# An attention and mixture-of-experts kernel on one core: the second group's second product turned round, zeros placed freely, and the engines' order planned with other durations

## The chip, the core and the metric

The kernel runs on one NeuronCore of a Trainium2 chip. The metric is the device time of one execution in microseconds; the number to be predicted is the median of the timed runs of the changed kernel.

## What is computed

Two steps in float32. First chunked attention: 4 batches, 8 heads, 768 positions, head dimension 64; every chunk of 32 queries sees 8 memory keys, 16 keys to its left, its own 32 and 8 to its right. Its output, 3072 rows (tokens) of 512, is the input of the second step, a dense mixture of 4 experts:

```python
scores = scale * np.matmul(q_c, k_full.transpose(0, 1, 3, 2))
a = np.exp(scores - np.max(scores, axis=-1, keepdims=True))
a = a / (np.sum(a, axis=-1, keepdims=True) + 1e-09)
out[:, :, c_start:c_end] = np.matmul(a, v_full)
...
p = domain_probs / (domain_probs.sum(-1, keepdims=True) + 1e-09)
for e in range(E):                       # E = 4
    h = np.maximum(x @ w1[e], 0.0)       # 3072 x 512 by 512 x 1024
    out += p[:, e:e + 1] * (h @ w2[e])   # 3072 x 1024 by 1024 x 512
```

## The kernel before

**Groups and experts.** A group is one batch, 768 tokens in two halves of 384. The work is numbered by n = 4 * group + expert, from 0 to 15. While a group is multiplied with the weights, attention of the next group runs between (`window`, `attend`): one unit is 96 queries, with a score product (L485), a mixing product (L618) and the softmax on VectorE (DVE) and ScalarE (ACT).

**Products.** Each float32 matrix is split into a high part (a cast to fp32r on ACT, L550) and a low part (what is left, a subtraction on DVE, L568, or on GpSimd (POOL), L569; `parts_of`). A product is three matmuls: high by high, high by low, low by high. From expert 1 on the first product (L883) is a Strassen-like product of seven half-sized products (named 11, 12, 6, 5, 7, 4, 3 after their steps), worked off in four pairs p of hidden blocks per expert; class `Full` takes the sums, rectifies them (`relu`, `direct`) and splits them again as operands of the second product.

**The second product** is again seven products of half size, in two forms. `Halves` (L1123) has the hidden layer's 128 tokens as the stationary operand and 256 output columns moving by: three token blocks t, so steps 10, 11, 12, 20 and so on; its sums are weighted with the routes p as they are added up (`add_up`, L837, 256 columns). `Across` (L1167) has the weights as the stationary operand and 384 tokens moving by: two steps t per product; the result stands with the model dimension on the partitions, so the routes are multiplied onto the hidden layer before (`weigh`, L983; for pairs 0 and 1 a rectification on ACT, L552, and a product on POOL or DVE), from a broadcast copy that `want_routes` loads, and the sums (384 columns) are plain additions. `FLAT` is the first group that uses `Across`. In `Halves` the steps 10 and 11 write PSUM banks of kind `a` (two of these) and 12 a bank of kind `moe` (three); in `Across` steps 10 and 11 both write kind `a`. The kind `a` banks also hold the first product's sums: the fourth pair's bank is read last after step 4 (`direct`: the rectification on ACT in groups with `Halves`, `weigh` on DVE in groups with `Across`). Step 3 of the fourth pair (product S4) comes between step 4 and the next step of the second product.

**The start.** The first group's attention and first products are laid out by hand in `FIRST_BLOCK`: S is a unit's scores, T its transposes (L1350), X its mixing (L1369), M and N first products (L817), g and G second products of the first expert (L863), and W n matmuls of zeros (L1270) on idle data, which keep TensorE (PE) at work.

**The order of the engines.** Nothing else is ordered by hand. `Plan` records every operation with its reads and writes. PE's order is that of the program; for ACT, DVE, POOL and the queue of SyncE (SP), which issues all DMAs, `run` draws orders at random around due times, replays each with modelled durations, and keeps the best; an addition or subtraction may be on DVE or POOL, a copy on ACT or DVE, as it finds best. There are three plans: the start ("first"), groups' work up to expert 3 ("mid"), and all from n = 4 on ("fin").

## Time and profile before

| what | value |
|---|---|
| timed runs | 1043.56, 1045.62, 1047.1 us (median 1045.62) |
| span of the profiled execution, first to last instruction | 1041.7 us |
| mean granted clock of PE | 0.997 |
| DMA moved | 300.88 MB, mean 289 GB/s |
| start (first plan) | 0 to 72.4 us |
| first group and expert 3 (mid) | to 305.8 us |
| second group, n = 4 to 7, `Halves` | 305.8 to 559.3 us |
| third and fourth group, n = 8 to 15, `Across` | 559.3 to 1038.3 us |

The profiled execution has no time of its own beside its span; the timed runs lie 1.9 to 5.4 us above it. In the profile, PE is the matmuls and PEld the weight loads beside them. A row of the timeline has the start, the length, the engine, the line, output and inputs, the shapes (a matmul's stationary operand, then its output) and how many instructions are merged; in square brackets stand the idle time before it and who ended it. A row of a group has busy time, mean length in ns, and idle time before with its releasers. Matmuls overlap in their pipeline, so that a matmul's length is longer than its distance to the next.

### The profile page before, as it was taken

The numbers are of one execution on the slowest core, as the hardware profiler recorded it, in microseconds if no ns is written. First come the engines' busy times: TensorE is split into PE (matmuls) and PEld (weight loads), VectorE is DVE, ScalarE is ACT, GpSimd is POOL, SyncE is SP. The second block draws the span as 40 slices with busy tenths as digits, with TensorE's granted clock in tenths as the row PEclk, the third lists the DMA queues.
The fourth block names the chain that finished last, engine by engine and source line by source line (L and its number), as shares of the span: only waits on it lengthen the run. The fifth ranks groups of instructions, "written<-read, shape, count | busy, mean of one in ns | idle before, by whom it ended". The sixth has DMA issues, their size and how long they took to land.

```text
span 1041.7 us, 21404 instructions
## 1 busy us (share of the span) xinstructions
PE 1030.7 (99%) x7899; PEld 988.8 (95%) x7899; DVE 809.4 (78%) x1358; ACT 539.3 (52%) x1426; POOL 464.9 (45%) x426
## 2 busy tenths in 40 slices
PE   7999999999999999999999999999999999999998
PEld 6988988989889999999999999999999999999998
DVE  6869786868976768678797968969699765949485
ACT  5636864746737656474755546445453534334241
POOL 2444654854605436172253606346072634626172
PEclk8999999999999999999999999999999999999999
DMA  9557989989979999999988878879679887879784
GB/s 297 179 206 238 376 335 359 357 333 352 347 279 384 357 306 333 326 342 328 309 259 303 282 259 278 279 246 296 232 241 305 287 262 247 280 237 275 250 253 144
DMA packets 185512, 300.88 MB, mean 289 GB/s; under 512 B 14816, under 2 KB 125504, under 8 KB 185408
## 3 DMA queue, kind: packets, MB, share of 16 engines
q1 hardware_dynamic: 185408, 299.51, 84.4%
q8 instruction: 63, 1.03, 0.4%
q14 instruction: 41, 0.34, 0.1%
HBM read 230.21 MB, written 69.26 MB: 287 GB/s over the span
## 4 chain that ended last, share of the span: by engine, by line
PE 93%; DVE 4%; DMA 1%; issue 1%; POOL 0%; ACT 0%; SPq 0%; DVEq 0%; POOLq 0%; ACTq 0%
PE a_ps L883 22%; PE moe_ps L883 16%; PE moe_ps L863 13%; PE a_ps L1167 12%; PE moe_ps L1167 10%; PE a_ps L1123 7%; PE moe_ps L1123 5%; PE moe_ps L817 3%; PE x_ps L618 2%; PE s_ps L485 2%; DVE A_lo L568 1%; DVE u L983 1%; DVE u L568 1%; DMA raw<-in_w_dram 1%; DMA qk_pair<-in_qk_dram 1%
## 5 line engine op out<-in xcount | busy, mean ns | idle before, releaser
L569 POOL TENSOR_TENSOR u<-u,routes 128x384 f32<-128x384 f32 x46 | 50.3, 1095 | 191.8 <-ACT u L552 191.5
L568 DVE TENSOR_TENSOR A_lo<-u,A_hi 128x384 fp32r<-128x384 f32 x139 | 118.2, 868 | 18.8 <-ACT A_hi L550 18.4
L863 PE MATMUL moe_ps<-w,h_hi 128*128 128x512 f32 x384 | 119.8, 393 | 0.0
L568 DVE TENSOR_TENSOR u<-moe_ps,u 128x384 f32<-128x384 f32 x120 | 66.2, 552 | 63.4 <-PE moe_ps L883 48.3
L569 POOL TENSOR_TENSOR raw<-raw 128x256 f32<-128x256 f32 x57 | 51.2, 899 | 127.1 <-DMA raw<-in_w_dram 83.1
L550 ACT COPY u<-a_ps 128x384 f32<-128x384 f32 x120 | 57.0, 475 | 78.8 <-PE a_ps L883 77.1
L550 ACT CAST A_hi<-u 128x384 fp32r<-128x384 f32 x144 | 73.3, 514 | 37.5 <-DVE u L983 31.1
L863 PEld LDWEIGHTS moe_ps<-w,h_hi 128*128 128x128 f32 x384 | 71.1, 188 | 14.8
L883 PE MATMUL a_ps<-xc_hi,ring 128*128 128x384 f32 x384 | 82.2, 336 | 0.0
L552 ACT ACTIVATE u<-u 128x384 f32<-128x384 f32 x96 | 50.2, 525 | 53.3 <-DVE u L568 52.7
L863 PE MATMUL moe_ps<-w,h_lo 128*128 128x512 f32 x192 | 75.0, 391 | 0.0
L569 POOL TENSOR_TENSOR us<-u,u 128x384 f32<-128x384 f32 x43 | 49.4, 1149 | 41.8 <-DVE u L983 20.3
L883 PEld LDWEIGHTS a_ps<-xc_hi,ring 128*128 128x128 f32 x384 | 67.8, 188 | 0.0
L1167 PE MATMUL a_ps<-A_hi,ring 128*128 128x384 f32 x256 | 65.8, 338 | 0.6 <-DVE u L983 0.6
L569 POOL TENSOR_TENSOR us<-u,us 128x384 f32<-128x384 f32 x43 | 49.5, 1151 | 30.2 <-DVE us L568 23.7
L569 POOL TENSOR_TENSOR u<-u,u 128x384 f32<-128x384 f32 x48 | 59.8, 1246 | 0.6
L569 POOL TENSOR_TENSOR u<-u,us 128x384 f32<-128x384 f32 x46 | 58.2, 1266 | 2.7 <-DVE A_lo L568 1.1
L639 ACT ACTIVATE s_sb<-s_ps,mx 96x64 f32<-96x64 f32 x192 | 57.1, 309 | 0.7
L568 DVE TENSOR_TENSOR acc<-a_ps,acc 128x384 f32<-128x384 f32 x52 | 28.8, 553 | 26.7 <-PE a_ps L1167 26.1
L883 PE MATMUL a_ps<-xc_lo,ring 128*128 128x384 f32 x192 | 48.9, 336 | 0.0
L1167 PEld LDWEIGHTS a_ps<-A_hi,ring 128*128 128x128 f32 x256 | 45.8, 188 | 2.4 <-DVE u L983 2.2
L569 POOL TENSOR_TENSOR w<-raw,w 128x512 fp32r<-128x512 f32 x25 | 35.9, 1443 | 26.7 <-ACT w L550 17.6
(237 smaller groups left out, 3110.8 us busy)
## 6 DMA issues: line engine op xcount, KB each, us to landing
ring<-k SPq DMA_DIRECT2D x144, 512.0 KB, 4.8
ring<-t SPq DMA_DIRECT2D x96, 512.0 KB, 6.0
ring<-w SPq DMA_DIRECT2D x72, 512.0 KB, 5.4
k<-w SPq DMA_DIRECT2D x48, 512.0 KB, 5.3
w<-w SPq DMA_DIRECT2D x32, 512.0 KB, 5.5
raw<-in_w_dram SPq DMA_DIRECT2D x62, 256.0 KB, 5.2
ring<-k SPq DMA_DIRECT2D x48, 256.0 KB, 4.1
qk_t<-in_qk_dram SPq DMA_DIRECT2D x24, 464.0 KB, 6.3
```

Source lines behind the costliest of these rows:

```text
L485: nc.tensor.matmul(s_ps.ap[c * CH:(c + 1) * CH, j * NPAIR + g, 0:KW], lhsT=x()[rows, g * UQ + c * CH:g * UQ + (c + 1) * CH], rhs=x()[rows, ...
L550: nc.scalar.copy(out(), x())
L552: nc.scalar.activation(out(), x(), func)
L568: ("DVE", t_dve(cols), lambda: nc.vector.tensor_tensor(out=out(), in0=x(), in1=y(), op=op)),
L569: ("POOL", t_pool(cols), lambda: nc.gpsimd.tensor_tensor(out=out(), in0=x(), in1=y(), op=op)),
L618: nc.tensor.matmul(x_out()[j * D:(j + 1) * D, g, :], lhsT=v_t.ap[:, h * D:(h + 1) * D], rhs=aT[:, j * NPAIR + g, :], start=True, stop=True,)
L639: now["plan"].add("ACT", t_act(KW) + 0.08, lambda h=h: nc.scalar.activation(s_sb.ap[:, h, :], s_in()[:, h, :], AF.Exp, bias=mx.ap[:, h, :] ...
L817: nc.tensor.matmul(ps.ap[:, lo:hi], lhsT=a[:, c * P:(c + 1) * P], rhs=x[:, c, lo:hi], start=(i == 0), stop=(i == len(steps) - 1),)
L863: nc.tensor.matmul(self.ps.ap, lhsT=h.ap[:, self.rows], rhs=w.ap[:, part, :], start=(i == 0 and k == 0), stop=(i == NF - 1 and k == 2),)
L883: nc.tensor.matmul(ps.ap[:, 0:SG], lhsT=a()[:, c * P:(c + 1) * P], rhs=y[:, k0 + c, :], start=(first and i == 0), stop=(i == len(steps) - ...
L1123: nc.tensor.matmul(ps.ap[:, cols], lhsT=x.ap[:, rows], rhs=w_ap[:, y, :], start=(begins and k == 0 and i == 0), stop=(k == NP2 - 1 and i = ...
L1167: nc.tensor.matmul(ps.ap[:, 0:SG], lhsT=w_ap[:, y, rows], rhs=x.ap, start=(begins and k == 0 and i == 0), stop=(k == NP2 - 1 and i == 2), ...
```

## The change

Four things change.

1. `FLAT` is 1 instead of 2: the second group (n = 4 to 7) uses `Across` too. The host puts the outputs of three groups, not two, back in order.
2. `FIRST_BLOCK` has other numbers and places of zeros (79 in all, before 98), in pieces of four, and another order of first products and transposes.
3. The planner's durations: latencies by engine and direction, the full wait of a DVE operation with two SBUF inputs for a running POOL operation and the other way round (`LOCK`), the end of an instruction hidden under the next (`OVER`), and single costs of PE and ACT work.
4. The planner plans in windows of 10 to 15 us with a limited sight instead of the whole plan at once, carries the state of three replays with it, and judges a window by PE's end and a little by the other engines'.

A way to fuse exponential and sum at the start (`FUSED`) is written but used by no unit.

```diff
-FLAT = 2
+FLAT = 1
...
-FIRST_TURNS, FIRST_SEED = 600, 1
+FIRST_TURNS, FIRST_SEED = 100, 1
 FIRST_BLOCK = """
-W32 S0 S1 S2 W6 S3 W30 T0 W6 X0 T1 W12 X1 S4 W12 M1 T3 M5 X3 M2 T2 S5 X2 S6 M6 N7 N5 N4 N6 N0 N2 T5 N1 N3 S7 X5
-g0 T4 g1 G0 X4 T7 G1 X7 T6 g2 X6 G2
+W31 S0 S1 W4 W4 S2 W4 W4 S3 W4 T0 W4 W4 W4 X0 T1 W4 W4 X1 W4 W4 S4 M6 M5 T3 M2 X3 T2 M1 X2 S5 S6 N1 N3 S7 N6 N7
+N4 N5 N0 T5 T4 N2 X4 g0 G0 X5 T7 g1 G1 T6 X7 g2 X6 G2
 """
...
-LATENCY = 0.12
-LATENCY_PE = 0.2
+LOCK = 0.14
+LATENCY = {"PE": 0.055, "ACT": 0.035, "DVE": 0.035, "POOL": 0.08, "SP": 0.12}
+BEYOND = {"PE": 0.165, "ACT": 0.0, "DVE": 0.0, "POOL": 0.0, "SP": 0.085}
+SELF = {"PE": 0.0, "ACT": 0.02, "DVE": 0.02, "POOL": 0.05, "SP": 0.12}
+OVER = {"PE": 0.0, "ACT": 0.1, "DVE": 0.08, "POOL": 0.04}
...
+HOPS = {"first": (15.0, 400.0, 60.0), "mid": (10.0, 160.0, 60.0), "fin": (10.0, 60.0, 30.0)}
+TRAIL = 0.05
...
 def t_pool(cols):
-    return 0.35 + cols * 0.0021
+    return 0.185 + cols * 0.00216
...
-                if op.two and start < pool_to:
-                    time += 0.9 * min(pool_to - start, time)
                 if op.two:
+                    time += max(0.0, pool_to - start - LOCK)
                     dve_to = start + time
             elif e == "POOL":
-                if start < dve_to:
-                    time += 0.25 * min(dve_to - start, time)
+                time += max(0.0, dve_to - start - LOCK)
                 pool_to = start + time
...
+                score = sum(f["PE"] + TRAIL * sum(max(0.0, f[e] - f["PE"]) for e in ("ACT", "DVE", "POOL"))
+                            for f, _ in ends) / len(ends)
...
-            pe(1.0, scores(s_ps, lambda: qk_t.ap), [qk_t], [s_ps])
+            pe(0.72, scores(s_ps, lambda: qk_t.ap), [qk_t], [s_ps])
...
-            now["plan"].add("ACT", t_act(KW) + 0.08, lambda h=h: nc.scalar.activation(
+            now["plan"].add("ACT", t_act(KW) + 0.147, lambda h=h: nc.scalar.activation(
...
-        pe(0.111 * n, fn, [], [])
+        pe(0.107 * n, fn, [], [])
```

The lines of the changed kernel are numbered anew: L1123 is L1204, L1167 is L1248, L883 is L964, L983 is L1064, L568 and L569 are L649 and L650.

What the change moves, at three places. The first is PE at the second product of the first expert of the second group (n = 4): the end of the third step of the fourth pair, product 1's step 10, steps 4 and 3 of the fourth pair, and the next step of product 1. `xa`, `xb` and `xc` are the parts of the input, `ring` the weights, `A_hi` and `A_lo` the parts of the hidden layer. Before:

```order
L883 MATMUL a_ps<-xc_lo,ring 128x384 x2
L1123 MATMUL a_ps<-ring,A_hi 128x256 x2
L1123 MATMUL a_ps<-ring,A_lo 128x256
...
L883 MATMUL a_ps<-xb_hi,ring 128x384 x4
L883 MATMUL a_ps<-xb_lo,ring 128x384 x2
L883 MATMUL moe_ps<-xb_hi,ring 128x384 x4
L883 MATMUL moe_ps<-xb_lo,ring 128x384 x2
L1123 MATMUL moe_ps<-ring,A_hi 128x256 x2
L1123 MATMUL moe_ps<-ring,A_lo 128x256
```

With the change:

```order
L964 MATMUL a_ps<-xc_lo,ring 128x384 x2
L1248 MATMUL a_ps<-A_hi,ring 128x384 x2
L1248 MATMUL a_ps<-A_lo,ring 128x384
...
L964 MATMUL a_ps<-xb_hi,ring 128x384 x4
L964 MATMUL a_ps<-xb_lo,ring 128x384 x2
L964 MATMUL moe_ps<-xb_hi,ring 128x384 x4
L964 MATMUL moe_ps<-xb_lo,ring 128x384 x2
L1248 MATMUL a_ps<-A_hi,ring 128x384 x2
L1248 MATMUL a_ps<-A_lo,ring 128x384
```

The step behind the fourth pair writes an `a` bank where it wrote a `moe` bank; operands change places and 256 columns become 384. In the whole program 1008 matmuls of 256 columns are gone and 672 of 384 have come.

The second place is PE in the first 25 us: scores (`qk_pair`), transposes of the bands (`band_107` for even units, `band_109` for odd ones), mixing (`v_t`), and the first products (`xa_hi`). The rows left out between them are the zeros: before, 6, 30, 6, 12 and (behind the fifth score) 12.

```order
L485 MATMUL att_ps<-qk_pair 32x64 x72
...
L485 MATMUL att_ps<-qk_pair 32x64 x24
...
L1350 MATMUL att_ps<-ident,band_107 128x96 x8
...
L1369 MATMUL x_ps<-aT_111,v_t 64x96 x8
L1350 MATMUL att_ps<-ident,band_109 128x96 x8
...
L1369 MATMUL x_ps<-aT_113,v_t 64x96 x8
L485 MATMUL att_ps<-qk_pair 32x64 x24
...
L817 MATMUL moe_ps<-xa_hi,w_359 128x192 x8
L817 MATMUL moe_ps<-xa_lo,w_359 128x192 x4
L1350 MATMUL att_ps<-ident,band_109 128x96 x8
```

With the change the zeros left out are 8, 8, 4, 12, 8 and 8:

```order
L566 MATMUL att_ps<-qk_pair 32x64 x48
...
L566 MATMUL att_ps<-qk_pair 32x64 x24
...
L1438 MATMUL att_ps<-ident,band_107 128x96 x8
...
L1457 MATMUL x_ps<-aT_111,v_t 64x96 x8
L1438 MATMUL att_ps<-ident,band_109 128x96 x8
...
L898 MATMUL moe_ps<-xa_hi,w_342 128x192 x8
L898 MATMUL moe_ps<-xa_lo,w_342 128x192 x4
L898 MATMUL moe_ps<-xa_hi,w_352 128x192 x8
L898 MATMUL moe_ps<-xa_lo,w_352 128x192 x4
L1438 MATMUL att_ps<-ident,band_109 128x96 x8
```

The third score stands behind eight zeros, four zeros instead of thirty stand in front of the first transpose, and two blocks of first products instead of one in front of the third transpose.

The third place is DVE in the last expert (n = 15), around the end of the fourth pair; `u11`, `u12`, `u21` and `u22` are sums of the first product, `A12_lo` and `A22_lo` low parts of the hidden layer, `acc` sums of the second product. Before:

```order
L568 TENSOR_TENSOR u22_12781<-a_ps_12705,u22_12781 128x384
L983 SCALAR_TENSOR_TENSOR u21_12674<-u21_12674,routes_12251 128x384
L983 SCALAR_TENSOR_TENSOR u22_12781<-u22_12781,routes_12251 128x384
L568 TENSOR_TENSOR A22_lo_12823<-u22_12601,A22_hi_12702 128x384
L983 SCALAR_TENSOR_TENSOR u12_12836<-a_ps_12705,routes_12215 128x384
```

With the change:

```order
L649 TENSOR_TENSOR u22_12436<-a_ps_12364,u22_12436 128x384
L649 TENSOR_TENSOR A12_lo_12471<-u12_12411,A12_hi_12421 128x384
L1064 SCALAR_TENSOR_TENSOR u22_12436<-u22_12436,routes_11958 128x384
L1064 SCALAR_TENSOR_TENSOR u21_12329<-u21_12329,routes_11958 128x384
L649 TENSOR_TENSOR acc_131<-a_ps_12458,acc_131 128x384
L1064 SCALAR_TENSOR_TENSOR u12_12495<-a_ps_12364,routes_11873 128x384
```

The last row of each is the weighing that frees the fourth pair's `a` bank; the lower part that stood right in front of it is another one further up, and a sum of the second product stands there now. Counted over the whole program, 44 low parts `A_lo` of 139 go from DVE to POOL, and of the sums and products with routes some 125 go from POOL to DVE or come new on DVE; DVE has 1342 rows with the change and 1294 before, POOL 430 and 431.

More of the change, by code (lines that the diff above doesn't have):

```diff
@@ L1 @@
 import random
+from bisect import bisect
 from contextlib import ExitStack
@@ new lines, in run, with judge @@
+        self.assign(self.ways)
+        free, dma, _, _, end = copies[0]
+        for op in ops:
+            op.end = end[op.index]
+        self.done = {**free, "DMA": dma}
+        self.score = self.judge([({**c[0], "DMA": c[1]}, max(c[4])) for c in copies])
+        self.emit(order)
+    def judge(self, ends):
+        total = 0.0
+        for free, most in ends:
+            if self.last:
+                total += most
+            elif not self.ahead:
+                total += free["PE"]
+            else:
+                total += max(free["PE"], free["SP"] + self.ahead, free["DMA"] + DMA_FIRST, *(free[e] - BEHIND for e in ("ACT", "DVE", "POOL")))
+        return total / len(ends)
@@ L266, in pushed @@
             for _ in range(rng.randrange(2, 14)):
-                need = [d for d in op.deps if d.engine != "PE"]
+                need = [d for d in op.deps if d.engine != "PE" and d in start]
                 if not need:
@@ L308, in replay, with schedule @@
-        return free["PE"] + (max(0.0, free["SP"] + self.ahead - free["PE"]) if self.ahead else 0.0)
-    def schedule(self, bias, ways):
+            else:
+                free[e] = start + time - OVER[e]
+            most = max(most, end[op.index])
+        return {**free, "DMA": dma}, most, (free, dma, pool_to, dve_to, end)
+    def schedule(self, place, base, bias, ways, stop, inside):
         self.assign(ways)
-        ops, wait = self.ops, self.wait
-        for op in ops:
+        wait = self.wait
+        waiting = {e: [] for e in ENGINES}
+        for op, left, ready in base:
@@ L324, in choose @@
+            waiting[op.engine].append(op)
+        for e in ENGINES[1:]:
+            waiting[e].sort(key=lambda o: (o.late, o.index))
+        free, at, line = dict(place["free"]), place["at"], self.line
+        dma, pool_to, dve_to, drift = place["dma"], place["pool_to"], place["dve_to"], place["drift"]
+        order, left = [], len(base)
+        everything = stop >= len(line)
         def choose(e, force):
```

188 lines of the change are left out of this document (119 added, 69 removed).

## The prediction

> **What bounds the kernel now.** I read the page first, then the waits of TensorE (PE), the windows, the timeline of PE at its stages, and last the groups by shape. The page's busy row and its chain of work:
>
> ```profile
> PE 1030.7 (99%) x7899; PEld 988.8 (95%) x7899; DVE 809.4 (78%) x1358; ACT 539.3 (52%) x1426; POOL 464.9 (45%) x426
> ...
> PE 93%; DVE 4%; DMA 1%; issue 1%; POOL 0%; ACT 0%; SPq 0%; DVEq 0%; POOLq 0%; ACTq 0%
> ```
>
> PE is busy for all but 11 us of the span of 1041.7 us, and it is 93% of the chain. So two things can shorten the kernel: fewer or cheaper matmuls, and the 11 us. The waits of PE and the windows say where these lie (after the stretch's length, the busy time of PE, PEld, DVE, ACT, POOL; then PE's granted clock):
>
> ```profile
> PE att_ps L485 <- DMA qk_pair<-in_qk_dram: 1.8, 1, 1.8
> PE att_ps L485 <- issue: 1.7, 1, 1.7
> PE x_ps L1369 <- ACT aT L563: 1.4, 2, 0.8
> PE x_ps L1270 <- POOL idle L455: 1.0, 1, 1.0
> PE att_ps L1350 <- ACT band L550: 0.6, 1, 0.6
> PE a_ps L1167 <- DVE u L983: 0.6, 2, 0.3
> PE att_ps L1350 <- POOL band L569: 0.3, 1, 0.3
> ...
> 0.00:20.00 20.00, 14.76 (x310) 13.17 (x310) 11.48 (x21) 8.81 (x17) 5.48 (x12) 0.83 0.87 275
> 20.00:40.00 20.00, 18.32 (x306) 16.90 (x304) 18.46 (x35) 16.75 (x37) 10.60 (x8) 1.00 0.79 283
> 40.00:80.00 40.00, 40.00 (x324) 35.33 (x324) 29.94 (x58) 14.22 (x28) 14.35 (x14) 1.00 0.47 168
> ```
>
> The first 40 us hold 6.9 us of PE's idle time; from 40 us on PE is full, but for 0.6 us at one kind of place (L1167) and the last sum's drain. Busy time hides waits shorter than a matmul's pipeline, so behind 40 us I go by distances from start to start.
>
> **The turn of the second product.** Two stretches of PE, one in the second group (256 columns) and one in the last (384):
>
> ```profile
> 349.73 0.40 PE L1123 MATMUL a_ps<-ring,Sb_hi 128*128 128x256 f32 x2
> ...
> 351.17 0.40 PE L1123 MATMUL a_ps<-ring,Sb_hi 128*128 128x256 f32 x2
> ...
> 1034.46 0.51 PE L1167 MATMUL moe_ps<-Sb_hi,ring 128*128 128x384 f32 x2
> ...
> 1036.54 0.51 PE L1167 MATMUL moe_ps<-Sb_hi,ring 128*128 128x384 f32 x2
> ```
>
> From the first to the second row lie 12 matmuls: (351.17 - 349.73)/12 = 0.120 us for 256 columns, (1036.54 - 1034.46)/12 = 0.1733 us for 384. By the code an expert has 7 products of 3 token blocks, 4 pairs and 3 terms, 252 matmuls of 256 columns; turned it has 7 x 2 x 4 x 3 = 168 of 384. Both stream 64,512 columns, and what is saved is the fixed part of 84 matmuls. For four experts: 1008 x 0.120 = 121.0 us go, 672 x 0.1733 = 116.5 us come: **-4.5 us**. PE is the chain there, so all of it counts.
>
> [...]
>
> What the turn lays on the other engines, by the groups of the second and third group's stretches:
>
> ```profile
> L837 DVE SCALAR_TENSOR_TENSOR acc<-a_ps,pr,acc 128x256 f32<-128x256 f32 x40 | 19.1, 477 | 7.0 <-PE a_ps L1123 6.7
> L983 DVE SCALAR_TENSOR_TENSOR u<-u,routes 128x384 f32<-128x384 f32 x24 | 19.0, 796 | 0.3
> L983 DVE SCALAR_TENSOR_TENSOR u<-a_ps,routes 128x384 f32<-128x384 f32 x16 | 8.8, 548 | 1.8 <-PE a_ps L883 1.8
> L568 DVE TENSOR_TENSOR acc<-a_ps,acc 128x384 f32<-128x384 f32 x26 | 14.3, 552 | 7.7 <-PE a_ps L1167 7.4
> ...
> 431.60:494.50 62.90, 62.90 (x551) 62.10 (x550) 48.06 (x89) 36.55 (x103) 27.40 (x27) 1.00 0.98 340
> 621.00:683.00 62.00, 62.00 (x468) 61.02 (x467) 50.10 (x86) 28.97 (x86) 26.66 (x24) 1.00 0.84 269
> ```
>
> Per expert of the second group the routes are now put on the hidden layer: 6 weighings of 0.80 us and 4 of 0.55 come to VectorE, and 18 adds of 0.48 become 12 of 0.55: +4.8 + 2.2 - 8.6 + 6.6 = +5.0 us on 48.1 us (the first row of windows), so 53 of 62 us. The third group has run like this with 50.1 us of VectorE, and PE is full in both rows. ScalarE loses 10 rectifications per expert; 6 products with the routes come, for GpSimd or VectorE as the planner likes. Two broadcasts of the routes per expert (192 KB each) pass SP's queue, 0.4 MB where 340 GB/s (the row's last number) move 21 MB in 62.9 us. Beside PE all of this is hidden and costs 0; the cover is VectorE's 9 free us per expert, and were it gone, each missing us would be one of PE's.
>
> **One hand-over loses its cover.** Behind the fourth pair, product 1's next step follows product S4. Before, that step wrote a free `moe` bank; turned, it writes the `a` bank that the fourth pair's A22 product has just filled, and waits until VectorE has weighed it out (the rows of PE's order in the section on the change). Groups three and four show the price:
>
> ```profile
> 833.10 1.37 DVE L568 TENSOR_TENSOR A_lo<-u,A_hi 128x384 fp32r<-128x384 f32 x1
> ...
> 834.20 0.51 PE L883 MATMUL moe_ps<-xb_lo,ring 128*128 128x384 f32 x2
> 834.39 0.54 DVE L983 SCALAR_TENSOR_TENSOR u<-a_ps,routes 128x384 f32<-128x384 f32 x1
> ...
> 834.99 0.44 PE L1167 MATMUL a_ps<-A_hi,ring 128*128 128x384 f32 x1 [0.28 <-DVE u L983]
> ```
>
> PE's two matmuls from 834.20 on need 0.35 us, the next starts after 0.79: a wait of 0.44 us, because a lower part of 1.37 us (a sum of its size takes 0.55) stands ahead of the weighing. The eight experts of groups three and four pay 1.45 us there in all, read in this way: three nothing, five 0.14 to 0.44, of which the first and the last are
>
> ```profile
> 712.96 0.51 PE L883 MATMUL moe_ps<-xb_lo,ring 128*128 128x384 f32 x2
> 713.50 0.61 PE L1167 MATMUL a_ps<-A_hi,ring 128*128 128x384 f32 x2
> ...
> 1010.17 0.51 PE L883 MATMUL moe_ps<-xb_lo,ring 128*128 128x384 f32 x2
> 1010.95 0.62 PE L1167 MATMUL a_ps<-A_hi,ring 128*128 128x384 f32 x2 [0.27 <-DVE u L983]
> ```
>
>  Twelve experts pay it after the change. Ends: the new order removes all of it, -1.4 us; every expert pays the worst, 12 x 0.44 - 1.45 = +3.8 us. For the last expert the new VectorE order has a sum of 0.55 us in front of the weighing where a lower part stood, which shortens it, while four experts are added to it: I take **0**.
>
> **The first 40 us.** Rows of the timeline, and the clock:
>
> ```profile
> 10.54 1.96 ACT L550 COPY band<-s_sb 32x64 f32<-32x64 f32 x4 [1.20 <-DVE s_sb L1316]
> 12.61 3.38 PE L1270 MATMUL x_ps<-idle 128*128 128x128 bf16 x30
> 15.79 0.97 PE L1350 MATMUL att_ps<-ident,band 96*128 96x96 f32 x8
> ...
> 23.03 1.11 PE L817 MATMUL moe_ps<-xa_hi,w 128*128 128x192 f32 x8
> 25.25 0.88 PE L1350 MATMUL att_ps<-ident,band 96*128 96x96 f32 x8 [0.63 <-ACT band L550]
> 30.08 0.88 PE L1350 MATMUL att_ps<-ident,band 96*128 96x96 f32 x8 [0.28 <-POOL band L569]
> ...
> 10.00:12.00 2.00, 0.55 (x27) 0.31 (x14) 1.72 (x3) 1.44 (x4) 0.00 (x0) 0.50 1.02 385
> ```
>
> The band of unit 0 is whole at 12.50 us, but thirty matmuls of zeros stand in front of its transpose, which starts at 15.79 us: 3.3 us late. They were meant for time that the wait without a releaser (1.7 us, just before) had used up. The change leaves 4 zeros there, and 12 behind it. Two waits follow later, 0.63 us ahead of the transpose at 25.25 and 0.28 ahead of that at 30.08; the new order puts one more block of first products (over 1.1 us, the row at 23.03) in front of each. If everything moves up with the transpose the head gains 3.3 + 0.9 = 4.2 us. If VectorE decides, it gains little: from 20 to 40 us it is busy for 18.46, so only 1.5 us can be squeezed there, and the band's multiplication now stands behind the third score's maximum. The low end is a loss of 0.5 us, when a stretch without zeros keeps the clock at 0.50 (the last row) a little longer. I take **-2.0**, the free 1.5 us and a part of what is idle before 20 us, nearer to VectorE's row than to the transpose's. The waits for the first loads (1.8), for an instruction without a releaser (1.7) and for the zeros' memset (1.0) stay.
>
> **The rest of the order.** The planner's new durations and windows move nearly every instruction off PE, 44 lower parts among them to GpSimd and some 80 sums back to VectorE. Where PE was full it can gain nothing, so the sign can only be a loss; the hand-over above bounds it. The drain behind the last matmul stays.
>
> **The rivals.**
> 1. *The turn alone counts.* The head is VectorE's, nothing comes of the zeros: -4.5, 1041.1 us. For it speaks 18.46 of 20 us; against it the two waits that are covered without VectorE.
> 2. *Hand-overs at their worst.* Twelve waits of 0.44 us: -4.5 - 2.0 + 3.8 = -2.7, 1042.9 us. Five of eight experts show such a wait now.
> [...]
> 4. *Slower: the bank of the hand-over.* Where the weighing stands behind a whole contended lower part (1.37 us) in each of twelve experts, PE waits 12 x 1.37 - 1.45 = 15.0 us more: 1045.6 - 6.5 + 15.0 = 1054.1 us. It eats the gain from (6.5 + 1.45)/12 = 0.66 us per hand-over on, and is slower by 0.3% from 0.92 us on. Against it: the worst of eight is 0.44.
>
> That the change does not do what it says is out: its order has no matmul of 256 columns left and 672 more of 384.
>
> **How the numbers follow.** -4.5 + 0 - 2.0 = -6.5 us, a span of 1035.2 us. The timed runs (1043.56 to 1047.1 us, median 1045.62) lie 1.9 to 5.4 us above the span; no time of the profiled execution's own is given, so I carry the difference over to the median: **1039.1 us**. Chances: the forecast 0.60, rival 1 0.16, rival 2 0.11, rival 3 0.04, rival 4 0.09. About 0.3% (3.1 us) is what a measurement of this kernel can tell from no change. The forecast and most of rival 1 are faster by more: 0.75; rivals 2 and 3 and the rest of 1 are within: 0.16; rival 4: 0.09. The range goes from the head's better end and half the hand-overs, 1036, to just past rivals 1 to 3, 1043.8.
>
> **What would show it.** Right: 384-column matmuls 0.173 us apart where the second group ran 0.120, that group's four experts together some 4 us shorter; the first transpose near 13 us, PE full some 2 us earlier; a total of waits at the hand-over of 0 to 3 us. Wrong: a first M product no earlier than 23 us (the head), waits over 0.66 us each for the weighing (rival 4), or waits of PE for other lower parts between 70 and 560 us, where now there are none.

## The result, and the profile after

The changed kernel takes **1049.6 us** (median of five runs, 1048.2 to 1050.0) beside 1044.4 us (1043.1 to 1047.1) of the kernel before on the same chip: a ratio of 1.0047, 95% interval 1.0032 to 1.0062. It is slower by some 5.2 us where the prediction had 6.5 us gained; the time lies above the range. The profiled execution took 1048.4 us and has a span of 1046.6 us, 4.9 us more than that of before.

The page of the changed kernel, the busy row and the chain of work:

```profile
PE 1027.9 (98%) x7544; PEld 982.4 (94%) x7544; DVE 811.7 (78%) x1391; ACT 525.2 (50%) x1384; POOL 487.2 (47%) x431
...
PE 74%; DVE 14%; DMA 5%; issue 3%; POOL 2%; ACT 1%; SPq 0%; DVEq 0%; ACTq 0%; POOLq 0%
```

PE has less work, as meant, but the chain is now PE for only 74% (93% before): 14% of it passes through VectorE and 5% through DMAs. The waits of PE (line waited for: us in total, times, longest) say at which places:

```profile
PE a_ps L964 <- DMA ring<-k: 3.1, 2, 2.4
PE att_ps L566 <- issue: 2.2, 1, 2.2
PE a_ps L1248 <- DVE u L1064: 2.2, 4, 1.2
PE x_ps L699 <- DVE aT L742: 1.5, 2, 1.3
PE att_ps L566 <- DMA qk_pair<-in_qk_dram: 1.1, 1, 1.1
PE a_ps L964 <- DVE u L649: 1.0, 2, 0.6
PE x_ps L1351 <- POOL idle L536: 1.0, 1, 1.0
PE moe_ps L1248 <- DVE acc L649: 0.8, 1, 0.8
```

Three of these rows belong to the start and were there before (the first loads, the memset, `issue`). New are the ring of weights and many kinds of waits for VectorE, between 300 and 900 us, where before had 0.6 us. By stages, from the first matmul of each (the second group from the first product of expert 4 to that of expert 8, and so on; a group's last products come behind the next one's first, so that before's second group ends here at 555.7 us and in the table ahead of the prediction at 559.3):

| stage | before | after | difference |
|---|---|---|---|
| start, to the first product of the second half | 72.4 | 69.3 | -3.1 |
| first group, to expert 4 | 233.4 | 236.1 | +2.7 |
| second group | 249.9 | 252.1 | +2.2 |
| third group | 245.5 | 249.4 | +3.9 |
| fourth group and drain | 240.5 | 239.7 | -0.8 |

The start did move. PE's timeline there, the first transposes and the first M product:

```profile
13.03 0.87 PE L1438 MATMUL att_ps<-ident,band 96*128 96x96 f32 x8
...
21.01 1.14 PE L898 MATMUL moe_ps<-xa_hi,w 128*128 128x192 f32 x8
```

They are 2.8 and 2.0 us earlier than before. At the end of the first group most of it is gone again:

```profile
302.63 0.39 PE L944 MATMUL moe_ps<-w,h_lo 128*128 128x512 f32 x1
305.41 0.98 PE L964 MATMUL a_ps<-xa_hi,ring 128*128 128x384 f32 x4 [2.39 <-DMA ring<-k]
```

PE is done with the first group at 303.0 us and waits 2.4 us for the first weights of the next; before, it came to this place at 305.8 us and found them there. The turned products run as forecast:

```profile
359.87 0.51 PE L1248 MATMUL a_ps<-Sa_hi,ring 128*128 128x384 f32 x2
...
361.43 0.51 PE L1248 MATMUL a_ps<-A_hi,ring 128*128 128x384 f32 x2
```

There are nine matmuls from the first row to the second, (361.43 - 359.87)/9 = 0.173 us each. So the second group's matmuls are 4.5 us shorter, and the group is 2.2 us longer: 6.7 us are lost in it beside the matmuls. For 5.0 us of these PE is idle in the windows below (the length less PE's busy time); its waits there are 0.7 us for the ring, 0.7 us for ScalarE and 3.6 us for VectorE. What the other engines do in groups two and three (windows; after the length the busy time of PE, PEld, DVE, ACT, POOL, then PE's clock, DMA share and GB/s), before:

```profile
305.83:555.74 249.91, 249.87 (x2182) 246.31 (x2181) 194.54 (x338) 148.58 (x410) 105.78 (x99) 1.00 0.95 325
555.74:801.21 245.47, 245.44 (x1811) 241.40 (x1809) 202.38 (x341) 122.83 (x349) 105.27 (x89) 1.00 0.84 273
```

and after:

```profile
305.41:557.52 252.11, 247.11 (x1845) 240.65 (x1845) 208.59 (x355) 129.24 (x355) 130.87 (x117) 1.00 0.97 328
557.52:806.91 249.39, 247.27 (x1810) 241.86 (x1809) 200.76 (x347) 126.65 (x360) 110.39 (x91) 1.00 0.84 267
```

In the second group VectorE has 14 us more and GpSimd 25 us more: 39 us, or 9.8 us per expert, where the prediction had counted 5.0 us on VectorE and left GpSimd's part without a price. This is busy time, in which operations of either engine also take longer beside the other's (VectorE's product with the routes at 402.36 us 3.84 us, the one at 407.62 us, while GpSimd rests, 0.56 us; GpSimd's `Sa_lo` at 599.00 us, through which VectorE works without a break, 2.20 us, the one at 402.83 us 1.01 us), and not all of it is the turn's: the new planner moves lower parts to GpSimd, where they take longer (1.18 us on average for 0.78 on VectorE), and the same group unturned has 312 to 337 us on the two in the four runs below that have the new planner, for 300 us before. The turn alone, with the old planner, brings it to 352 us, 12.8 us more per expert:

```profile
304.40:565.40 261.00, 249.58 (x1845) 241.56 (x1845) 215.60 (x349) 128.95 (x355) 136.00 (x123) 0.99 0.94 318
```

The third group, which was taken as the proof that a turned group runs without waits, had 308 us on the two together before; the turned second group has 340 us, and its DMAs are full (0.97 against 0.84; 0.95 in the second group of before). What the second group has and the third has not are the sums of weights that experts 4 to 6 make for later products (`raw`). The groups of VectorE and of GpSimd in the second group after:

```profile
L649 DVE TENSOR_TENSOR raw<-raw 128x256 f32<-128x256 f32 x16 | 10.0, 624 | 1.7 <-POOL raw L650 1.6
L649 DVE TENSOR_TENSOR raw<-raw,t_hi 128x512 fp32r<-128x512 f32 x9 | 7.7, 859 | 0.1
...
L650 POOL TENSOR_TENSOR raw<-raw 128x256 f32<-128x256 f32 x16 | 14.0, 875 | 9.1 <-DVE raw L649 6.0 <-DMA raw<-in_w_dram 2.9
L650 POOL TENSOR_TENSOR raw<-raw,t_hi 128x512 fp32r<-128x512 f32 x7 | 9.0, 1289 | 7.3 <-ACT t_hi L631 6.9 <-DVE raw L649 0.4
```

10.0 + 7.7 + 14.0 + 9.0 = 40.7 us of work (38.3 us in the kernel before), nothing of which runs in groups three and four.

### The profile page after: what moved, and what is told of

Read it like the earlier page. It is cut to its first block, busy times and chain, and to the rows that moved or that the text cites. A ratio compares the mean times of both kernels' runs of the same rounds, so it can differ in the third digit from the quotient of the medians.

```text
span 1046.6 us, 20702 instructions
## 1 busy us (share of the span) xinstructions
PE 1027.9 (98%) x7544; PEld 982.4 (94%) x7544; DVE 811.7 (78%) x1391; ACT 525.2 (50%) x1384; POOL 487.2 (47%) x431
## 4 chain that ended last, share of the span: by engine, by line
PE 74%; DVE 14%; DMA 5%; issue 3%; POOL 2%; ACT 1%; SPq 0%; DVEq 0%; ACTq 0%; POOLq 0%
PE a_ps L964 16%; PE a_ps L1248 16%; PE moe_ps L1248 13%; PE moe_ps L964 12%; PE moe_ps L944 10%; PE moe_ps L898 3%; DVE u L649 3%; DVE u L1064 2%; DMA ring<-k 2%; DVE A_lo L649 2%; PE x_ps L699 1%; DMA t<-raw 1%; PE s_ps L566 1%; DVE us L649 1%; DVE aT L742 1%
## 5 line engine op out<-in xcount | busy, mean ns | idle before, releaser
L650 POOL TENSOR_TENSOR A_lo<-u,A_hi 128x384 fp32r<-128x384 f32 x49 | 57.5, 1177 | 111.9 <-ACT A_hi L631 110.7
L649 DVE TENSOR_TENSOR u<-moe_ps,u 128x384 f32<-128x384 f32 x120 | 66.0, 550 | 52.8 <-PE moe_ps L964 40.0
L1248 PE MATMUL a_ps<-A_hi,ring 128*128 128x384 f32 x384 | 98.6, 338 | 3.0 <-DVE u L1064 2.2
L650 POOL TENSOR_TENSOR u<-u,routes 128x384 f32<-128x384 f32 x37 | 39.5, 1068 | 108.1 <-ACT u L633 99.5
L964 PE MATMUL a_ps<-xc_hi,ring 128*128 128x384 f32 x384 | 82.4, 337 | 0.0
L649 DVE TENSOR_TENSOR A_lo<-u,A_hi 128x384 fp32r<-128x384 f32 x95 | 74.0, 784 | 6.7 <-ACT A_hi L631 5.8
L1248 PEld LDWEIGHTS a_ps<-A_hi,ring 128*128 128x128 f32 x384 | 69.0, 188 | 5.1 <-DVE u L1064 3.9
L649 DVE TENSOR_TENSOR acc<-a_ps,acc 128x384 f32<-128x384 f32 x78 | 42.7, 550 | 32.9 <-PE a_ps L1248 32.8
L964 PEld LDWEIGHTS a_ps<-xc_hi,ring 128*128 128x128 f32 x384 | 67.7, 188 | 0.5 <-ACT u L631 0.2
L1248 PE MATMUL a_ps<-A_lo,ring 128*128 128x384 f32 x192 | 64.5, 336 | 0.0
L1064 DVE SCALAR_TENSOR_TENSOR u<-u,routes 128x384 f32<-128x384 f32 x72 | 57.9, 814 | 0.2
L649 DVE TENSOR_TENSOR u<-a_ps,u 128x384 f32<-128x384 f32 x60 | 33.1, 551 | 29.1 <-PE a_ps L964 25.9
L1248 PE MATMUL a_ps<-Sa_hi,ring 128*128 128x384 f32 x192 | 49.7, 340 | 0.7 <-ACT Sb_hi L631 0.7
L1248 PE MATMUL moe_ps<-Sa_hi,ring 128*128 128x384 f32 x192 | 49.0, 337 | 0.8 <-DVE acc L649 0.8
L649 DVE TENSOR_TENSOR acc<-moe_ps,acc 128x384 f32<-128x384 f32 x66 | 35.8, 549 | 17.4 <-PE moe_ps L1248 17.2
```

The lines of the kernel that those rows point to most:

```text
L649: ("DVE", t_dve(cols), lambda: nc.vector.tensor_tensor(out=out(), in0=x(), in1=y(), op=op)),
L650: ("POOL", t_pool(cols), lambda: nc.gpsimd.tensor_tensor(out=out(), in0=x(), in1=y(), op=op)),
L964: nc.tensor.matmul(ps.ap[:, 0:SG], lhsT=a()[:, c * P:(c + 1) * P], rhs=y[:, k0 + c, :], start=(first and i == 0), stop=(i == len(steps) - ...
L1064: dve(lambda: nc.vector.scalar_tensor_tensor(out=u.ap, in0=x(), scalar=0.0, in1=r.ap, op0=ALU.max, op1=ALU.mult), SG, [r], [u] + keys, two ...
L1248: nc.tensor.matmul(ps.ap[:, 0:SG], lhsT=w_ap[:, y, rows], rhs=x.ap, start=(begins and k == 0 and i == 0), stop=(k == NP2 - 1 and i == 2), ...
```

## The experiments

My first theory was **A**: the planner's new rules leave no margin and make the waits, since the third group, whose matmuls did not change, lost most. Its rivals were **B**, the turn itself makes them, and **C**, each order is a draw of a search at random, and draws differ. Each run below was timed in the same job as the kernel before; the differences are between those medians. "Second group" and "third group" are read from each run's own trace as in the table above.

### What part of the change does it

**The turn alone**:

```diff
-FLAT = 2
+FLAT = 1
```

> The kernel before with FLAT = 1 and nothing else: old zeros, old durations, the whole plan searched at once. Theory A (the new plan has no margin and makes the waits): the turn gives its -4.5 us, 1040 us beside 1044.4 of before, or 1042.5 if the routes' broadcasts ahead of the ring cost 2.5 us at 302 us whoever plans. Theory B (the turn itself makes the waits: weighings on VectorE, the bank of the hand-over, the broadcasts): 1046 to 1049 us, since the second group had 6.7 us of new waits and the boundary 2.5 us against 4.5 saved. Theory C (luck of a search at random): anything from 1038 to 1048.

1055.5 us, +10.6 (ratio 1.0102, interval 1.0087 to 1.0117). The second group took 261.0 us. In this draw the old rules lose twice as much with the turn as the new ones.

**The change without the turn** (`FLAT = 2` in the changed kernel):

> The changed kernel with FLAT = 2: new zeros and new planning, the second group with 256 columns as before. Theory A: the new waits of groups two and three stay (about 4 us each), the start keeps its -3.1 us and the turn's -4.5 us are lost, 1047 to 1053 us. Theory B: the waits go with the turn, the start's gain stays, 1041 to 1043 us. C: anything between.

1046.2 us, +1.3 (1.0007 to 1.0024); second group 254.4, third 245.2 us.

**The old rules from the second plan on**, the rest as changed: a second planner class holds the old `run`, `replay`, `schedule` and durations and plans "mid" and "fin".

```diff
-    plan = now["plan"] = Plan(free, ends)
+    plan = now["plan"] = OldPlan(free, ends)
```

> The turn and the new start (its zeros and its plan by the new rules) as in the changed kernel, but the second and third plan (from 72 us on) by the old durations, the old contention rule and the search over the whole plan. Theory A: -3.1 and -4.5 us without new waits, 1036.8 us, up to 1039.5 if the broadcasts cost their 2.5 us at 302 us; faster than both kernels. Theory B: start -3.1, turn and its waits +2 to +5, 1043 to 1047 us. C: 1034 to 1046.

1048.5 us, +3.6 (1.0028 to 1.0053); second group 250.0, third 249.9 us.

**The start alone** (the same, with `FLAT = 2`):

> The new start as in the changed kernel, the second group not turned, the second and third plan by the old rules. Theories A and B: the start's -3.1 us alone, 1041.3 us. C (a search from another state scatters by several us): 1038 to 1046.

1047.0 us, +2.1 (1.0008 to 1.0027), where -3.1 was expected. Its start is 2.8 us shorter than before's (69.6 us), and its first group 3.0 us longer (236.4): the timeline of PE there,

```profile
302.83 0.39 PE L1146 MATMUL moe_ps<-w,h_lo 128*128 128x512 f32 x1
305.96 1.17 PE L1166 MATMUL a_ps<-xa_hi,ring 128*128 128x384 f32 x4 [2.74 <-DMA ring<-k]
```

is the wait of the changed kernel, without the turn and its broadcasts. **Theory A falls** as the main cause: with the old rules the two turned kernels lie 3.6 and 10.6 us above before, with the new rules and no turn the time is 1.3 us above it. B stands, but not whole, for two kernels without the turn are slower too.

### What in the turn

Now the question was what of the turn makes the waits: **L**, its load on VectorE and GpSimd (the weighing), or **G**, the geometry (which bank a step writes, the order of the products). All four are made from the turn alone with the old rules, or from before.

**The turn without its weighing**:

```diff
-            self.k, self.routes = operands, routes
+            self.k, self.routes = operands, routes if n >= 2 * E else None
```

> The kernel before with FLAT = 1 (as the turn alone, 1055.5 us), but the second group's hidden layer is not weighed with the routes: its rectifications stay on ScalarE, as without the turn; the products with the routes are left out there, the broadcasts stay. [...] Theory G (what the turn does to the banks and the order of the products makes them): the waits stay, over 1050 us. Theory C (luck of the search): 1040 to 1055 without a pattern by group.

1047.1 us, +2.4 (1.0009 to 1.0029): 8 us less than with the weighing, yet 5 us above the 1042 us that I took for the upper end if the weighing made the waits (a second group of 246 to 247 us). Its second group took 254.3 us. Three of its waits and the clock made most of that: 1.7 and 2.2 us for the ring in expert 4, 3.4 us at clock 0.50 behind the second of these (some 1.6 us lost), and this wait at 548.9 us, which the waits put down to `issue` (timeline of VectorE and GpSimd, then of PE):

```profile
545.77 2.12 POOL L569 TENSOR_TENSOR xc_lo<-xr,xc_hi 128x768 fp32r<-128x768 f32 x1
548.22 0.54 DVE L568 TENSOR_TENSOR acc<-a_ps,acc 128x384 f32<-128x384 f32 x1
...
548.87 0.60 PE L1167 MATMUL a_ps<-Sa_hi,ring 128*128 128x384 f32 x2 [2.52 <-issue]
```

The profile names no releaser. By the times, PE's next bank is given free by the addition at 548.22 us, which ends 0.11 us before PE goes on and stood behind two subtractions of VectorE that took 3.44 us together, while GpSimd ran this operation of 2.12 us.

**The weighing without the turn** (`want_routes` for every group, in the kernel before):

```diff
-routes = [want_routes(n, half) for half in range(2)] if across else None
+routes = [want_routes(n, half) for half in range(2)]
```

> The kernel before (256 columns in the second group) with the routes put on the second group's hidden layer as well, so that they are multiplied in twice there: the turn's work for VectorE and GpSimd without the turn. Theory L: the second group grows from 249.9 us by 5 to 15 us of waits, 1050 to 1060 us. Theory G: nothing changes, 1044 to 1046 us. C: within 2 us of before.

1057.6 us, **+12.9** (1.0108 to 1.0137). Not one matmul differs from before, and the second group takes 260.0 us for 249.9, with 7.7 us of idle time of PE for 0.04. Its first three experts:

```profile
304.40:370.79 66.39, 62.65 (x538) 60.60 (x537) 53.22 (x90) 36.33 (x102) 30.76 (x27) 1.00 0.99 345
370.79:435.47 64.68, 63.13 (x551) 62.03 (x549) 48.91 (x85) 30.73 (x88) 36.11 (x32) 1.00 0.93 315
435.47:501.50 66.03, 63.61 (x551) 62.18 (x550) 59.07 (x102) 32.22 (x92) 38.88 (x37) 1.00 0.93 314
```

VectorE and GpSimd have 84 to 98 us together in experts that took 61 to 63 us before. So the load makes such waits with banks and order as before; G alone is not the cause. It is one draw, and since the sums keep their routes here, VectorE's part is 7.0 us per expert by the prediction's prices and not 5.0; but none of the eight unturned draws below loses more than 7.5 us. That G adds nothing is not shown by this run; the end of the experiments comes back to it.

**The turn without the weights' sums** (in `make2_combined`, for the experts that the second group serves; loads and stores stay):

```diff
+        if e >= 2:
+            for i, r in enumerate((r0, r1)):
+                k = kept2("t2", e, i)
+                dma(lambda k=k: k[:, p, 0], lambda r=r: r.ap, P * DM * 4, [r], [("t2", e, i, p, 0)])
+                dma(lambda k=k: k[:, p, 1], lambda r=r: r.ap, P * DM * 4, [r], [("t2", e, i, p, 1)])
+            return
```

> The turn alone, but the eight sums of weights that experts 4 to 6 make beside the products are left out (the four sums, the high parts and the subtractions; their loads and stores stay, of unsummed weights). Theory L: their 40 us of VectorE and GpSimd were what the third group does not have; experts 4 to 6 lose nearly all of their waits (5.2, 0.5 and 3.6 us), the seventh keeps its 6 us: 1046 to 1049 us. Were the DMAs the cause, 1055 as with the turn alone. Theory G: 1053 to 1056 us.

1048.6 us, +3.9 (1.0021 to 1.0046), as L had it, but not where L had it: experts 5 to 7 run in 63.0, 62.0 and 62.0 us, expert 4 still takes 67.2.

**The turn, another seed** (`plan.run(seed=2, last=True)`):

> The turn alone with another seed for the search of the last plan. Theory L with a search that hits more or less well: waits of 9 to 19 us in groups two and three together, 1046 to 1056 us, in any case not faster than before. Theory C: it may as well be 1040 us, since the first draw was a bad one.

1050.9 us, +6.2 (1.0051 to 1.0089), 4.6 us under the first draw. (Its trace is of its longest run, 1055.3 us.)

### The traffic, and the draw

Expert 4 kept its waits when only arithmetic was taken away. The new suspect was **D**: the DMAs are full there. In before too, where PE does not wait for it, the ring of nine loads starts empty at 302 us and catches up:

```profile
330.00:340.00 10.00, 10.00 (x67) 10.00 (x67) 8.23 (x15) 8.33 (x29) 5.21 (x5) 1.00 1.08 368
```

**The turn without the sums and without their traffic** (`COMBINED_M` and `COMBINED_E` empty; the later products take unsummed weights):

```diff
-COMBINED_M = {4: 1, 5: 1, 6: 2}
-COMBINED_E = {4: 1, 5: 1, 6: 2}
+COMBINED_M = {}
+COMBINED_E = {}
...
                     kind, half, o = self.PARTS[x]
+                    kind = "w2" if n % E >= 2 else kind
```

> The turn alone with its weighing, without the eight sums of weights of experts 4 to 6 and without their loads and stores. Beside the run that left out the sums but kept their DMAs (1048.6 us, 67.2 us in expert 4): theory D (the ring of weights comes late because the DMAs are full) says expert 4 falls to about 62 us and all to 1042 to 1044 us; theory L alone says no change beside that run, 1047 to 1049 us.

1044.1 us, +0.2 (0.9991 to 1.0009), a time as D had it. The second group:

```profile
305.99:367.08 61.09, 60.05 (x453) 58.46 (x452) 48.81 (x79) 32.75 (x94) 27.76 (x23) 1.00 0.97 329
367.08:428.68 61.60, 61.60 (x465) 60.68 (x465) 44.64 (x76) 28.48 (x84) 28.40 (x25) 1.00 0.84 271
428.68:490.28 61.60, 61.60 (x465) 60.68 (x465) 50.04 (x87) 29.54 (x87) 25.87 (x22) 1.00 0.83 269
490.28:552.54 62.26, 62.26 (x466) 60.79 (x466) 54.98 (x90) 30.81 (x75) 27.43 (x23) 1.00 0.84 274
```

246.6 us, 3.4 less than before, weighing and all, and two experts without a wait. Expert 4 falls from 67.2 to 61.1 us and its DMA share from

```profile
304.92:372.14 67.22, 62.41 (x454) 59.94 (x452) 47.05 (x80) 32.03 (x94) 25.41 (x22) 0.97 1.03 362
```

(the run that kept the traffic) to 0.97. The third group hides the gain: it takes 249.7 us for 245.5, with the same matmuls. So **the turn's saving is real, and the second group does not run without waits with all that the turn brings**: with the weighing alone it nearly does, with the weighing, the sums and their traffic it does not. But the 6 us of expert 4 are not D's. In the run that kept the traffic, PE's waits in expert 4 are

```profile
PE a_ps L1173 <- DVE u L989: 2.0, 1, 2.0
PE a_ps L889 <- DMA ring<-k: 1.7, 2, 1.4
PE a_ps L889 <- ACT u L550: 1.0, 1, 1.0
```

and behind the first of these, the hand-over at 343.8 us, the clock fell to 0.50 for 3.4 us (some 1.6 us lost). Without the traffic 0.6 us for the ring and 0.5 us at the hand-over are left. Only about 1 us of the difference is a wait for DMAs; the rest is the hand-over, ScalarE and the clock in another draw.

**The turn with both taken away**:

> The turn alone, with all that the second group has beside it taken away: it is not weighed with the routes, and the eight sums of weights that experts 4 to 6 make are left out with their loads and stores (the later products take unsummed weights). If the turn's -4.5 us of TensorE are real and only the load beside it (theory L for VectorE and GpSimd, theory D for the DMAs, which are full from 310 to 350 us) hides them: second group 245.4 to 246.5 us beside 249.9, in all 1040 to 1042.5 us. [...] Theory G: waits at the hand-over stay, 250 us and more.

1045.1 us, +1.1 (1.0002 to 1.0022); second group 247.9 us, of which 1.9 us are waits in expert 4, most of them for the ring. The group's gain is there; the total is not what I expected, since the third group takes 247.9 us for 245.5.

**Before with another seed**, nothing else changed (`plan.run(seed=2, last=True)`):

> The kernel before with another seed for the search of the last plan, nothing else. If the order found before is an ordinary draw: 1043 to 1046 us. If it is a good one, and any change that makes the search start anew costs (theory C): 1046 to 1049 us, with waits of 2 to 4 us in the second and third group where before had none.

1047.9 us, **+3.9** (1.0025 to 1.0050). The third group takes 248.5 us; its waits and those behind it are all of one kind, the hand-over:

```profile
PE a_ps L1167 <- DVE u L983: 2.8, 5, 1.4
```

Before has 0.6 us of it. **C holds as well**: the order of the kernel before is a good draw.

**The start with one of the weights' sums earlier**. In the start alone the ring's first load stood, in the SyncE queue, behind the last stores of these sums (the last store at 300.01 us, the ring at 300.43); theory **S** was that this holds the start's gain back.

```diff
-COMBINED_A = (2, 2, 2, 2)
+COMBINED_A = (3, 2, 2, 1)
```

> The new start alone (1047.0 us), with one of the sums of weights of expert 3 made in expert 0 instead (3, 2, 2, 1 for 2, 2, 2, 2). Theory S (the start's gain is given back at 303 us, because the ring's first load waits for the last store of these sums and not for TensorE): the ring is issued by 298 us, expert 4 starts at 303 to 304 us instead of 306, and the time is 1043.5 to 1045 us. Otherwise 1046 to 1048 us as with the start alone.

1044.9 us, +1.0 (1.0004 to 1.0021), 2.1 us under the start alone. The wait for the ring is gone,

```profile
305.18 0.39 PE L1146 MATMUL moe_ps<-w,h_lo 128*128 128x512 f32 x1
305.41 0.86 PE L1166 MATMUL a_ps<-xa_hi,ring 128*128 128x384 f32 x4
```

but the ring is issued at 299.7 us, not by 298, and expert 4 starts at 305.4 us, not at 303 to 304: the first group lost 0.7 us at another place, and this execution's start took 71.0 us.

### Is there an order without the waits

Still open was whether the turned group can have a good order at all.

**Before and the turn alone, searched for 400 turns instead of 100** (`TURNS = 400`):

> The kernel before, its second and third plan searched for 400 turns instead of 100. Theory C (orders are draws, and before's is a good one): 1043 to 1048 us, four times the search does not surely help since the model that judges an order does not see the waits. If 100 turns were simply too few: 1041 to 1043 us.

1047.9 us, +3.5 (1.0021 to 1.0045).

> The turn alone with the search of 400 turns. Theory L+D (the second group has too much for VectorE, GpSimd and the DMAs once it is weighed): 1048 to 1054 us, the second group stays over 250 us, whatever the search. Theory C: a good draw exists, second group 246 to 248 us and 1039 to 1043 us.

1051.3 us, +6.9 (1.0052 to 1.0077); second group 251.2 us. Four times the search helps neither. That the model which judges an order does not have the waits in it would explain this, but no run shows what the model itself expected.

**The changed kernel with another seed** for its last plan:

> The changed kernel with another seed for the search of its last plan. Theory L+D: 1048 to 1053 us as the other turned kernels (1048.5 to 1055.5 us). Theory C: it may be 1040 to 1046 us.

1048.4 us, +4.0 (1.0020 to 1.0043). (Its trace is of its shortest run, 1043.5 us.)

**The change without the turn, with the sums earlier**, 3, 2, 2, 1:

> The changed kernel without the turn (1046.2 us), and with the sums of weights at 3, 2, 2, 1 in experts 0 to 3, so that the ring is not late at 303 us. Theory S: the 1.1 us of waiting for the ring there go, 1044 to 1045.5 us; an ordinary draw of the second group may shift it by 2 us either way. Were it under 1042 us it would beat both kernels.

1045.7 us, +1.3 (1.0003 to 1.0028): no wait for the ring, but 2 us of new waits in the first group (237.1 us). S stays half a theory: the ring's wait can be taken away, the gain of the start has not been kept with that.

**The change without the turn, another seed, and with a longer sight** (`"fin": (20.0, 120.0, 60.0)`):

> The changed kernel without the turn (1046.2 us), with another seed for the last plan. All six orders of the group as it was, drawn anew, lie at 1044.9 to 1047.9 us, all six of the turned group at 1048.4 to 1055.5. If the turned group's load is the cause: this one too lies under 1048 us. In that run the fourth group took 239.4 us beside 240.5 of before and the third 245.2; with a better draw of the second (254.4 us there, 249.9 before) it would reach 1041 to 1043 us and beat both kernels.

1047.5 us, +3.6 (1.0020 to 1.0042).

> The changed kernel without the turn, with windows of 20 us and a sight of 120 us in the last plan for 10 and 60. If the short sight makes the waits of its second group (4.5 us there): 1041 to 1043 us. If the sight does not matter: 1045 to 1048 us, as the other orders without the turn.

1051.4 us, +7.5 (1.0058 to 1.0084). The short sight is not what makes the waits. And my clean line between kernels with and without the turn falls with this run; what is left is a difference of means. No version with the whole computation beat the kernel before.

All runs with the whole computation, difference to before in us, and the second and third group in their traces:

| kernel | difference | second | third |
|---|---|---|---|
| before | 0 | 249.9 | 245.5 |
| without the turn: start and sums earlier | +1.0 | 251.2 | 246.8 |
| change without turn | +1.3 | 254.4 | 245.2 |
| the same, sums earlier | +1.3 | 251.7 | 246.3 |
| start alone | +2.1 | 251.8 | 246.4 |
| before, longer search | +3.5 | 250.7 | 247.4 |
| change without turn, other seed | +3.6 | 251.4 | 248.8 |
| before, other seed | +3.9 | 251.0 | 248.5 |
| change without turn, longer sight | +7.5 | 256.6 | 248.9 |
| with the turn: old rules, new start | +3.6 | 250.0 | 249.9 |
| changed kernel, other seed (its shortest run's trace) | +4.0 | 250.1 | 245.7 |
| changed kernel | +5.2 | 252.1 | 249.4 |
| turn alone, other seed (its longest run's trace) | +6.2 | 256.6 | 249.8 |
| turn alone, longer search | +6.9 | 251.2 | 250.0 |
| turn alone | +10.6 | 261.0 | 248.1 |

The eight orders without the turn, drawn anew, lie 3.0 us above before on average, the six with it 6.1 us. So a new draw costs about 3 us, and the turn about 3 us more on average, where its matmuls save 4.5: some 7.6 us of waits come with it. These are means of few draws, five of the eight and three of the six with the new start, and the two sets overlap (+1.0 to +7.5 and +3.6 to +10.6).

The traces themselves bear the load out, and show that it is not all. The second group's busy time of VectorE and GpSimd together, and the idle time of PE there:

| kernels | the two engines, us | PE idle, us |
|---|---|---|
| before, its two new draws, the two unturned runs with the new start and the old planner | 296 to 308 | 0 to 0.6 |
| unturned, new planner (four) | 312 to 337 | 0.4 to 3.1 |
| turned, whole (six) | 339 to 352 | 2.9 to 11.4 |
| unturned, weighing put on | 355 | 7.7 |
| turned without the sums and their traffic | 308 | 1.0 |
| turned without the sums | 310 | 6.0 |
| turned without the weighing | 308 | 6.5 |
| turned with neither weighing nor sums and traffic | 254 | 2.0 |

The highest loads have the most idle time. But the turned group waits 1 to 6.5 us also where its load is that of before or less. In these four runs most of the idle time is for the ring and the hand-over, but for 2.5 us of `issue`. So the turn seems to make some waits without its load, as D and G have it; no run takes these apart.

## Why the prediction was wrong

- **The turn's matmuls, -4.5 us**: right. The spacing is 0.173 us, and the second group without the sums and their traffic took 246.6 us, of which 0.6 and 0.4 us are waits by its waits of PE. The smaller fixed part of a matmul that rival 3 stands for (0.04 in the chances, a place in the range) is shown by no run; what the traces show is 0.120 us for 256 columns and 0.173 us for 384.
- **"Beside PE all of this is hidden and costs 0; the cover is VectorE's 9 free us per expert"**: this is the step that failed. It counted 5.0 us on VectorE and gave GpSimd's part no price; both together got 12.8 us per expert with the old planner and 9.8 with the new one. It took the free time of one engine for cover, though single operations of VectorE and GpSimd take longer beside each other (3.84 us for 0.56, 2.20 for 1.01), and it took the third group as the example, which has neither the 41 us of weights' sums nor full DMAs. The weighing put on an unturned group costs 12.9 us, its new draw included; taking the weighing, the sums, the sums with their traffic, or all of these from the turned group (old rules, +6.2 to +10.6 us in three draws) leaves +2.4, +3.9, +0.2 and +1.1 us. The prediction's condition for a loss, "were it gone", was not the one that counts: VectorE still has 43.5 of 252.1 us free in the changed kernel's second group, and PE waits all the same, since single results come late.
- **The hand-over, 0 with ends of -1.4 and +3.8 us**: inside its ends. From start to start, the waits there in the changed kernel are 0.38, 1.35, 0.51, 0.30 and 0.62 us, 3.2 us beside 1.45 before, so +1.7. Rival 4, the only one on the slow side, had its sign right and its size not: of twelve places one has such a wait (1.35 us), and seven have none. Its mechanism does occur in other orders, up to 3.1 us at one place in the turn alone. The first of the five, 0.38 us, is this (timelines of GpSimd, VectorE and PE); the weighing at 401.89 us, which frees the bank, stood behind a sum of VectorE that took 1.21 us:

```profile
401.51 1.35 POOL L650 TENSOR_TENSOR s_sb<-s_sb,sm 96x512 f32<-96x512 f32 x1
...
401.76 0.51 PE L964 MATMUL moe_ps<-xb_lo,ring 128*128 128x384 f32 x2
401.89 0.54 DVE L1064 SCALAR_TENSOR_TENSOR u<-a_ps,routes 128x384 f32<-128x384 f32 x1
...
402.36 3.84 DVE L1064 SCALAR_TENSOR_TENSOR u<-u,routes 128x384 f32<-128x384 f32 x1
...
402.49 0.62 PE L1248 MATMUL a_ps<-A_hi,ring 128*128 128x384 f32 x2 [0.21 <-DVE u L1064]
...
402.83 1.01 POOL L650 TENSOR_TENSOR Sa_lo<-us,Sa_hi 128x384 fp32r<-128x384 f32 x1
...
403.81 1.00 POOL L650 TENSOR_TENSOR A_lo<-u,A_hi 128x384 fp32r<-128x384 f32 x1
...
404.76 1.01 POOL L650 TENSOR_TENSOR u<-u,u 128x384 f32<-128x384 f32 x1
```

- **The start, -2.0 us**: right in size, and lost behind. In nine traces with the new start the second half's first product begins at 68.8 to 71.9 us (mean 70.1), in eleven with the old at 70.8 to 73.2 (mean 71.8): -1.7. The table's -3.1 for the changed kernel may partly be the clock: in the profiled execution of before TensorE ran 6.8 us of the first 20 at clock 0.50, in that of the changed kernel 3.4 us (means of 0.83 and 0.91 there). Yet expert 4 begins at 305.6 us on average in both sets of traces: where PE is there earlier, it waits for the ring or at another place of the first group. The prediction asked what is late next for VectorE in the first 40 us, and not at the plan's end.
- **"Where PE was full it can gain nothing, so the sign can only be a loss; the hand-over above bounds it"**: the sign was right, the bound was not one. A new order moved every instruction of three engines, and the loss of a new draw, without any other change, measured 3.9 us (in its trace the second group is 1.1 us longer, the third 3.0). That is where the third group's +3.9 us have their like: seven of the eight orders without the turn show +0.8 to +3.4 us there too.
- **What would make it wrong**: the last sign named there, waits of PE between 70 and 560 us, came, 7.3 us in all; but none of them is for a lower part: 3.1 us are for the ring, the others for transposes and sums of VectorE, a weighing and a high part of ScalarE. The sign stood in the text without a price and without a chance.

What is not settled: how much of the second group's loss is VectorE and GpSimd, how much the DMAs and how much the turn's banks and order, since no run took away the traffic alone, no run changed the load with the order kept, and each run is another draw with some 3 us of its own.

## What to carry to other kernels

An engine that is free for a seventh of a stage was no cover here, where its operations took up to 3.84 us for 0.56 beside another engine's: add up both, and the DMAs, for that very stage, and look for what the stage you take as an example does not have. The sum is a warning and no threshold: in the turn without the sums expert 7 has 87 us on the two engines and no wait of PE, expert 4 has 72 us and 4.8 us of waits. Where the order comes from a search, an edit also buys a new draw: time the old kernel with other seeds first, and put the spread into the range. A gain at the start of a kernel counts only if what comes next, the loads of the next stage among it, can move up too.

## What was not expected of the hardware

**One operation of VectorE ended only behind four of GpSimd.** The operation at 402.36 us above takes 3.84 us (the same one at 407.62 us, while GpSimd rests, 0.56 us). It began while GpSimd ran the first operation shown, and ended at 406.20 us, 0.43 us behind the third after that one (404.76 + 1.01 = 405.77 us); GpSimd's took 1.00 and 1.01 us each. The new planner's rule (`LOCK`) has an operation wait for the one that is running when it begins, and for no other. By that the wait would have ended at 402.9 us (401.51 + 1.35); here it lasted through three more, so that the planner could not see such waits coming. Of all traces one more has such a row, in the third group of the change without the turn and with a longer sight (GpSimd, VectorE, PE):

```profile
725.65 1.95 POOL L650 TENSOR_TENSOR u<-u,us 128x384 f32<-128x384 f32 x2
...
722.00 6.03 DVE L649 TENSOR_TENSOR Sb_lo<-us,Sb_hi 128x384 fp32r<-128x384 f32 x1
...
728.41 0.55 DVE L649 TENSOR_TENSOR acc<-moe_ps,acc 128x384 f32<-128x384 f32 x1
...
729.01 0.62 PE L1248 MATMUL moe_ps<-Sa_hi,ring 128*128 128x384 f32 x2 [2.02 <-DVE acc L649]
```

GpSimd ran six operations without a break from 721.73 to 727.60 us; VectorE's ended 0.43 us behind the last, as above, and the addition behind it released PE after 2.02 us of waiting. No other VectorE operation of the twenty traces takes more than 2.9 us, so that such rows are rare.

**Behind some waits of 1.3 to 2.7 us the clock was 0.50 for 3.4 us.** In the run of the start alone, after the 2.74 us of waiting for the ring (windows of 1 us; the clock is the number behind the five engines):

```profile
306.00:307.00 1.00, 1.00 (x5) 1.00 (x6) 0.93 (x2) 0.00 (x0) 0.00 (x0) 0.77 1.01 357
307.00:308.00 1.00, 1.00 (x5) 1.00 (x4) 0.00 (x0) 0.20 (x1) 0.00 (x0) 0.50 1.02 413
...
309.00:310.00 1.00, 1.00 (x5) 1.00 (x4) 0.23 (x1) 0.00 (x0) 0.00 (x0) 0.52 1.02 411
```

Eleven matmuls ran 0.320 us apart instead of 0.173: 11 x 0.147 = 1.6 us on top of the wait. Behind 60 us the twenty traces have fourteen waits of PE of 1.8 to 3.0 us; 3.4 us at clock 0.50 followed six of them, among them the 2.20 us in the turn without weighing, and not the others, among them the 2.39 us of the changed kernel (clock 1.00 from 305.41 to 312 us) and the longest, 2.97 us in the turn alone. Once they followed a wait of only 1.31 us (at 345.7 us in the change without the turn and with a longer sight). What decides which of these waits the half clock follows, no run shows.
